# A banded attention and gated MLP on one core: the third tile's probabilities go through the DMA crossbar, and the low words of the weights are shifted in place

## The chip, the core and the metric
The kernel runs on one core of a Trainium2 chip. The core has TensorE (matmuls; "PE" in the profile, its weight loads "PEld"), VectorE (DVE), ScalarE (ACT), GpSimd (POOL) and SyncE (SP, which here only issues DMAs). They run at the same time and wait for each other by semaphores. SBUF is the working memory, PSUM the memory that TensorE writes. The metric is the device time of one execution in microseconds, median of the runs. Lower is better.

## What is computed
```
q, k, v: (8, 8, 576, 64)           # batch, heads, sequence, head size
scores = q @ k.T / sqrt(64) + slope[head] * -(i - j)     # only where 0 <= i - j < 128
attn   = softmax(scores) @ v       # (sum + 1e-9 in the denominator)
x      = attn as (4608, 512)       # tokens by heads * head size
h      = x @ w_in                  # (4608, 2048)
P = a0 + a1*h + a2*h^2 + a3*h^3
Q = 1 + |b0|*|h| + |b1|*h^2
out    = (P / (Q + 1e-6)) @ w_out  # (4608, 512), float32
```
All inputs and the output are float32, but w_in and w_out reach the kernel as 64-bit words (float64), which it converts itself.

## The kernel before
**Tiles.** The 4608 tokens are 36 blocks of 128 and 18 tiles of two blocks. Attention goes in steps: step j belongs to tile j // 2, and handles two of its four pairs of heads; one such pair is a "unit" (L508). A step's scores are 32 small matmuls (L466), 128 keys each, the window's two halves in `sc` and `side`; VectorE merges them (L491), adds the bias and takes the row maximum (L532), ScalarE takes the exponential and its sum (L537), VectorE the reciprocal of the sum (L544, L545), GpSimd scales (L546). The scaled probabilities `pr` must be transposed before the product with v (L417), which TensorE does in the same block as the next step's scores (L484).

**The transposition, in three ways (L563 to L591).** With j below DIRECT, TensorE transposes `pr` by four matmuls with a unit matrix (L561) and three operations pick from PSUM: ScalarE L580, VectorE L581 and L582. With j from DIRECT to below TURNED, TensorE transposes, ScalarE copies the whole (L586), and GpSimd makes the two parts (L589, L590). From TURNED on, ScalarE writes `pr` as two planes of 16-bit words (L566), SyncE issues a transposing DMA (L568: the crossbar), ScalarE puts the words together again (L569), and GpSimd makes the two parts. Before, step 4 goes the first way, step 5 the second, steps 6 to 35 the third.

**The weights (L608).** There are 32 pieces of 128 x 512 (16 of w_in, 16 of w_out), which arrive as `raw` of 512 KB, two 32-bit words an element, low and high. ScalarE turns the high words' exponent (a Prelu in place, L628). The low words are shifted right by 29 into a PSUM tile `cv` (L629), by ScalarE or by VectorE as the planner decides. VectorE shifts the high words left by 3 and joins the two (L630). The first tile uses these float32 weights. For the others each piece is split in a high and a low part: ScalarE casts (L642), VectorE or GpSimd subtracts (L643).

**The MLP (L649).** For two chunks of 128 of the 2048 columns at a time: up-projection (L667), the ratio P / Q by ScalarE (Abs L681, the affine part of P L686 or L697, Ln L690 or L701, Exp L691 or L702), GpSimd (Q: L683, L687 or L698) and VectorE (L688 to L707), then down-projection (L724), which adds up all 16 chunks in two PSUM banks `acc`. Lines L685 to L695 are the first tile's.

**The order.** Every operation is entered with a due time, the engines that may do it with a cost for each, and what it reads and writes (L98). The planner (L118) goes through a modelled time and gives each free engine the ready operation that is due first; the outcome is one fixed order for each engine (L780), which the chip's engines follow, each waiting where an operand isn't there. The due times come from constants (L297 to L304). VectorE's and GpSimd's operations marked `sb=True` are planned as excluding each other in time (L211, L231). The first tile's chunks, the conversions and splits and the first attention steps lie within the first 130 us. Small matmuls on constants (L760) fill TensorE until 19 us.
```
    if j >= TURNED:
        planes = slot(sb2, [P, 2, 4 * P], U16, "planes")
        turned = slot(sb2, [P, 8, P], U16, "turned")
...
    else:
        plan.op(A + (D2 if t else D0), {"p": 28 + 108 * 4}, transpose, ...)
```
Of the kernel before, what the change touches and what calls it, by code (L numbers as in the profile page):

```python
# [11 lines left out]
F32 = mybir.dt.float32  # L12
F32R = mybir.dt.float32r
BF16 = mybir.dt.bfloat16
I32 = mybir.dt.int32
U32 = mybir.dt.uint32
U16 = mybir.dt.uint16
AF = mybir.ActivationFunctionType
ALU = mybir.AluOpType
PSUM = bass.MemoryType.PSUM  # L20

P = 128
B, H, S, D = 8, 8, 576, 64
NT, DM, FF = B * S, H * D, 2048
# [10 lines left out]
MASKED = -8.0e9  # L35
GUARD = 1.0 + 1e-6
EARLY = 0
DIRECT = 5
TURNED = 6


def block_type(n):
# [239 lines left out]
def banded_attention_ratio_mlp(ctx: ExitStack, tc: tile.TileContext, kqv, w_in, w_out, ab, bias, ident, out):  # L282
    nc = tc.nc
# [6 lines left out]
    ps4 = ctx.enter_context(tc.tile_pool(name="ps4", bufs=4, space=PSUM))  # L290
# [3 lines left out]
    NJ = 2 * NTILE  # L294


    A0, DA, T0, L0, L1 = -20.125, 1.042, 19.836, 59.132, 26.846  # L297
    AOFF, D2, D3, JL, VL = -0.9676, 4.293, 7.221, 11.472, 6.149
    SP, SV, SA, SG, LL = 0.000768, 0.2712, 0.1218, 0.4427, 2.857
    ML, ZA, ME, OE, C0 = 24.839, 1.199, 1.338, 10.451, 0.4053  # L300
    DC, CO, DO, WL, S0 = 3.813, 18.57, 3.877, 4.536, 80.884
    DS, SL, AW, BL, VE = 1.477, 8.756, 26.824, 0.9349, 13.143
    DU, V0, DL, B2, B3 = 0.7375, 2.733, 1.877, 23.544, 56.47
    FE, D0, D4 = 19.023, 0.5665, 1.663  # L304

    plan = Plan({"p": 1000 * SP, "v": 1000 * SV, "a": 1000 * SA, "g": 1000 * SG})

    def slot(pool, shape, dtype, name, tag=None, view=None):
        return Slot(pool, count[id(pool)], shape, dtype, name, tag or name, view)

    def ap(s):
        if s.ap is None:
            s.ap = s.pool.tile(s.shape, s.dtype, name=s.name, tag=s.tag)
        return s.ap

    def act(n, psum, ptr=0):
        return (67 if psum else 105) + 0.833 * n + 95 * ptr
# [16 lines left out]
    guard, low_bias, tiny = fixed[:, 0:1], fixed[:, 1:2], fixed[:, 2:6]  # L334
# [38 lines left out]
    def c_time(k):  # L373
        return C0 + DC * (k // 2) if k % 2 == 0 else CO + DO * (k // 2)
# [133 lines left out]
    def unit(j, i, A, main, mk, pt, v):  # L508
# [53 lines left out]

        if j >= TURNED:  # L563
            planes = slot(sb2, [P, 2, 4 * P], U16, "planes")
# [10 lines left out]
        mixed = lambda: fresh(0)  # L575
        if j < DIRECT:
            picked = lambda y: slant(pt(), y)
# [6 lines left out]
            return  # L584
        if j < TURNED:
            plan.op(A + D2 + 0.2, {"a": act(4 * P, 1)}, lambda e: nc.scalar.copy(ap(w)[:, : 4 * P].rearrange("q (k h c) -> q k h c", k=2, h=2), pt()), reads=pk, writes=[(w, 0)])  # L586
# [21 lines left out]
    def convert(k):  # L608

        c, m = k // 2, k % 2  # L610
        f = slice(P * c, P * (c + 1))
        raw = raws[k] = slot(const, [P, 2 * DM], I32, f"raw{k}", tag=f"hi{k % NL}")
        bits = w32[c, m] = slot(const, [P, DM], F32, f"w32_{c}_{m}", tag=f"w{c}_{m}")
        T = c_time(k)
        cv_s = slot(ps4, [P, DM], I32, "cv", tag="h")
        ck = (cv_s, 0)
        cv = lambda: ap(cv_s)
        words = lambda: ap(raw).rearrange("p (a w) -> p a w", w=2)
        top, low = (lambda: words()[:, :, 1]), (lambda: words()[:, :, 0])

        def load(e):
            if m == 0:
                eng[e].dma_start(words().rearrange("p (k f) w -> p k f w", k=NKC), w_in[:, f, :].rearrange("(k p) f w -> p k f w", p=P))
            else:
                eng[e].dma_start(words(), w_out[f, :, :])

        plan.op(T - WL, {"s": 1450}, load, writes=[(raw, 0), (raw, 1)], after=1000 * (T - WL - 4), follows=[raws[k - NL]] if k >= NL else ())
        plan.op(T, {"a": 575}, lambda e: nc.scalar.activation(top().bitcast(F32), top().bitcast(F32), AF.Prelu, scale=2.0**-112, alpha=-(2.0**32)), writes=[(raw, 0)])  # L628
        plan.op(T, {"a": 640, "v": 603}, lambda e: nc.scalar.activation(cv(), low().bitcast(U32), AF.Relu, bias=low_bias, scale=2.0**-29) if e == "a" else nc.vector.tensor_single_scalar(cv(), low(), 29, op=ALU.logical_shift_right), reads=[(raw, 1)], writes=[ck])  # L629
        plan.op(T + 1, {"v": 603}, lambda e: nc.vector.scalar_tensor_tensor(ap(bits).bitcast(I32), top(), 3, cv(), ALU.logical_shift_left, ALU.bitwise_or), reads=[(raw, 0), ck], writes=[(bits, 0)])  # L630

    def split(c, m):

# [132 lines left out]
    for k in range(2 * NFC):  # L766
        convert(k)
# [62 lines left out]
```

## Time and profile before

| what | value |
|---|---|
| median of 3 runs | 978.71 us (977.4 to 979.03) |
| the profiled execution's own time | 978.76 us |
| its span, first to last instruction | 977.0 us |
| TensorE busy (share of the span) | 957.9 us (98%) |
| VectorE busy | 780.3 us (80%) |
| ScalarE busy | 704.0 us (72%) |
| GpSimd busy | 500.3 us (51%) |
| chain that ended last: TensorE's share | 38%, of it L724 18% and L667 17% |
| mean granted TensorE clock | 0.997 |

An engine's busy time says how long it had an instruction; for matmuls, which overlap, the ends are modelled. The granted clock is the share of TensorE's full speed that it was allowed. A row of the timeline gives start, duration, engine, line, operation, result <- operands, how many in a row, and in brackets how long the engine was idle before and what ended it. Two records of L724 or L667 in the first tile are one matmul in full float32. A line number is that of the kernel before; in the changed kernel the lines from L629 on stand one lower.

### The profile page before, as it was taken

What the parts mean: (1) busy time and instruction counts of PE and PEld (TensorE: products, weight loads), DVE (VectorE), ACT (ScalarE), POOL (GpSimd) and SP (SyncE); (2) the same over time, 40 slices, a digit from 0 to 9 for tenths busy, and PEclk for the clock granted to TensorE, in tenths of its full rate; (3) what the DMA queues carried; (4) which work ended last, traced back from release to release, by engine and by line L of the source; (5) the groups of instructions that cost most, each with busy time, mean ns of one, the idle gap of its engine ahead of it and who ended that gap; (6) DMA issues with size and microseconds to landing.
All of it is one profiled execution on the core that took longest, in us unless ns stands there. A gap on an engine that the chain in (4) does not pass through costs nothing. (4 is left out here: it accounts for less than half of the span.)

```text
span 977.0 us, 25069 instructions
## 1 busy us (share of the span) xinstructions
PE 957.9 (98%) x9838; PEld 846.8 (87%) x9838; DVE 780.3 (80%) x1803; ACT 704.0 (72%) x1482; POOL 500.3 (51%) x502
## 2 busy tenths in 40 slices
PE   9898999999999999999999999999999999999998
PEld 7665888899999999999898989989899999999997
DVE  6799888877788878787887778877887788878776
ACT  5888877777677777777767777777777776777653
POOL 0327774555455554555555545545555545554542
PEclk9999999999999999999999999999999999999999
DMA  8991213333333332232332333433222332321100
GB/s 277 363 337 53 77 46 91 79 77 93 78 88 81 89 77 84 70 98 78 82 80 52 71 103 77 93 77 77 71 71 78 77 84 64 92 72 45 23 22 21
DMA packets 117861, 89.57 MB, mean 92 GB/s; under 512 B 68848, under 2 KB 101872, under 8 KB 117744
## 3 DMA queue, kind: packets, MB, share of 16 engines
q1 hardware_dynamic: 117744, 87.98, 33.0%
q8 instruction: 77, 1.26, 0.6%
q14 instruction: 40, 0.33, 0.1%
HBM read 62.79 MB, written 9.44 MB: 74 GB/s over the span
## 5 line engine op out<-in xcount | busy, mean ns | idle before, releaser
L667 PE MATMUL h<-x_hi,hi 128*128 128x256 f32 x1088 | 308.5, 284 | 1.5 <-DVE x_lo L436 1.5
L667 PE MATMUL h<-x_lo,hi 128*128 128x256 f32 x1088 | 306.4, 282 | 0.0
L667 PE MATMUL h<-x_hi,lo 128*128 128x256 f32 x1088 | 306.2, 281 | 0.0
L667 PEld LDWEIGHTS h<-x_lo,hi 128*128 128x128 f32 x1088 | 205.3, 189 | 31.4 <-issue 0.7
L667 PEld LDWEIGHTS h<-x_hi,hi 128*128 128x128 f32 x1088 | 205.6, 189 | 20.7 <-issue 3.3
L724 PE MATMUL acc<-hi,g_h 128*128 128x512 f32 x544 | 215.5, 396 | 1.4 <-ACT o L752 1.4
L724 PE MATMUL acc<-lo,g_h 128*128 128x512 f32 x544 | 214.8, 395 | 0.0
L667 PEld LDWEIGHTS h<-x_hi,lo 128*128 128x128 f32 x1088 | 205.6, 189 | 0.0
L724 PE MATMUL acc<-hi,g_l 128*128 128x512 f32 x544 | 198.0, 399 | 1.3 <-DVE g_l L707 1.2
L683 POOL TENSOR_SCALAR g_q<-g_u,babs 128x512 f32<-128x512 f32 x136 | 107.5, 791 | 168.5 <-ACT g_u L681 157.6
L546 POOL TENSOR_TENSOR pr<-pr,st 128x512 f32<-128x512 f32 x70 | 78.7, 1127 | 221.2 <-DVE st L545 131.5
L698 POOL TENSOR_TENSOR g_q<-g_q,g_u 128x512 f32<-128x512 f32 x136 | 178.2, 1311 | 19.9 <-ACT g_q L683 10.8
L704 DVE SCALAR_TENSOR_TENSOR g_h<-h,ab_sb,g_u 128x512 fp32r<-128x512 f32 x136 | 101.4, 746 | 68.7 <-ACT g_u L702 68.3
L699 DVE TENSOR_TENSOR g_p<-h,g_p 128x512 f32<-128x512 f32 x136 | 93.5, 688 | 64.1 <-ACT g_p L697 50.3
L681 ACT ACTIVATE g_u<-h 128x512 f32<-128x512 f32 x144 | 86.1, 598 | 77.4 <-PE h L667 45.6
L537 ACT ACTIVATE pr<-pr,st 128x128 f32<-128x128 f32 x288 | 111.9, 391 | 39.8 <-DVE st L532 39.7
L697 ACT ACTIVATE g_p<-h,ab_sb 128x512 f32<-128x512 f32 x136 | 105.7, 779 | 45.0 <-PE h L667 44.7
L701 ACT ACTIVATE g_u<-g_q,fixed 128x512 f32<-128x512 f32 x136 | 98.3, 724 | 44.1 <-POOL g_q L698 43.9
L700 DVE SCALAR_TENSOR_TENSOR h<-g_p,ab_sb,h 128x512 f32<-128x512 f32 x136 | 102.3, 752 | 19.7 <-ACT g_u L681 17.8
L724 PEld LDWEIGHTS acc<-hi,g_h 128*128 128x128 f32 x544 | 102.6, 189 | 9.6 <-ACT o L752 1.8
L705 DVE SCALAR_TENSOR_TENSOR g_q<-g_q,g_h 128x512 f32<-128x512 f32 x136 | 105.9, 780 | 5.7
L724 PEld LDWEIGHTS acc<-hi,g_l 128*128 128x128 f32 x544 | 100.3, 188 | 11.1 <-DVE g_l L707 2.2
(82 smaller groups left out, 1561.6 us busy)
## 6 DMA issues: line engine op xcount, KB each, us to landing
kq<-in_kqv SPq DMA_DIRECT2D x72, 320.0 KB, 3.6
v<-in_kqv SPq DMA_DIRECT2D x144, 128.0 KB, 3.8
out<-o SPq DMA_DIRECT2D x34, 256.0 KB, 2.0
raw<-in_w_in SPq DMA_DIRECT2D x16, 512.0 KB, 8.5
raw<-in_w_out SPq DMA_DIRECT2D x16, 512.0 KB, 8.7
bias_t<-in_bias SPq DMA_DIRECT2D x44, 64.0 KB, 2.8
turned<-planes SPq DMA_TRANSPOSE x60, 3.1
out<-o SPq DMA_DIRECT2D x4, 128.0 KB, 1.7
```

What stands on the lines that cost most here:

```text
L537: nc.scalar.activation(ap(pr)[:, :, y, :], ap(pr)[:, :, y, :], AF.Exp, bias=ap(st)[:, y : y + 1], scale=-1.0, accum_out=ap(st)[:, 4 + y : ...
L667: nc.tensor.matmul(h(n), w[:, k, :], x[:, k, :], start=(k == 0 and m == 0), stop=(k == NKC - 1 and m == len(seq) - 1))
L681: plan.op(E, {"a": act(W, 1)}, lambda e: nc.scalar.activation(v(g_u), v(h_s), AF.Abs), reads=[(h_s, 0)], writes=[(g_u, 0)])
L683: lambda e: nc.scalar.activation(v(g_q), v(g_u), AF.Identity, bias=ap(babs)[:, 0:1], scale=ap(babs)[:, 1:2]) if e == "a" else nc.gpsimd.te ...
L697: plan.op(E, {"a": act(W, 1, 2) - 20}, lambda e: nc.scalar.activation(v(g_p), v(h_s), AF.Identity, bias=ap(ab_sb)[:, 2:3], scale=ap(ab_sb) ...
L698: plan.op(E, {"g": ttc}, lambda e: nc.gpsimd.tensor_tensor(v(g_q), v(g_q), v(g_u), ALU.mult), reads=[(g_q, 0), (g_u, 0)], writes=[(g_q, 0) ...
L699: plan.op(E, {"v": dve(W)}, lambda e: nc.vector.tensor_tensor(v(g_p), v(h_s), v(g_p), ALU.mult), reads=[(h_s, 0), (g_p, 0)], writes=[(g_p, ...
L700: plan.op(E, {"v": dve(W, 1)}, lambda e: stt(v(h_s), v(g_p), ap(ab_sb)[:, 1:2], v(h_s), ALU.add, ALU.mult), reads=[(h_s, 0), (g_p, 0), (ab ...
L701: plan.op(E, {"a": act(W, 0, 1)}, lambda e: nc.scalar.activation(v(g_u), v(g_q), AF.Ln, bias=guard, scale=1.0), reads=[(g_q, 0)], writes=[ ...
L704: plan.op(E, {"v": dve(W, 1)}, lambda e: stt(v(g_h), v(h_s), ap(ab_sb)[:, 0:1], v(g_u), ALU.add, ALU.mult), reads=[(h_s, 0), (g_u, 0), (ab ...
L705: plan.op(E, {"v": dve(W)}, lambda e: stt(v(g_q), v(g_q), GUARD, v(g_h).bitcast(F32), ALU.add, ALU.mult), reads=[(g_q, 0), (g_h, 0)], writ ...
L724: nc.tensor.matmul(ap(accs[t][i]), x[:, sl], w, start=(c == 0 and part == 0 and m == 0), stop=(c == NFC - 1 and part == parts - 1 and m == ...
```

## The change
Three things change.

DIRECT and TURNED become 4: steps 4 and 5, the third tile's, are transposed by the crossbar, as the later ones were.

In the conversion ScalarE's exponent pass writes to the PSUM tile `cv` instead of in place, the low words are shifted in place in SBUF, by VectorE alone, with `sb=True` and a planned cost of 336 instead of 603 ns, and VectorE joins `cv` with the shifted words.

All constants of the due times are others, so the planner's order differs on every engine and throughout.

```
--- before.py
+++ after.py
@@ -35,8 +35,8 @@
 MASKED = -8.0e9
 GUARD = 1.0 + 1e-6
 EARLY = 0
-DIRECT = 5
-TURNED = 6
+DIRECT = 4
+TURNED = 4
 
 
 def block_type(n):
@@ -294,14 +294,14 @@
     NJ = 2 * NTILE
 
 
-    A0, DA, T0, L0, L1 = -20.125, 1.042, 19.836, 59.132, 26.846
-    AOFF, D2, D3, JL, VL = -0.9676, 4.293, 7.221, 11.472, 6.149
-    SP, SV, SA, SG, LL = 0.000768, 0.2712, 0.1218, 0.4427, 2.857
-    ML, ZA, ME, OE, C0 = 24.839, 1.199, 1.338, 10.451, 0.4053
-    DC, CO, DO, WL, S0 = 3.813, 18.57, 3.877, 4.536, 80.884
-    DS, SL, AW, BL, VE = 1.477, 8.756, 26.824, 0.9349, 13.143
-    DU, V0, DL, B2, B3 = 0.7375, 2.733, 1.877, 23.544, 56.47
-    FE, D0, D4 = 19.023, 0.5665, 1.663
+    A0, DA, T0, L0, L1 = -22.674, 0.3976, 18.443, 59.244, 25.804
+    AOFF, D2, D3, JL, VL = -1.431, 3.98, 7.461, 11.098, 6.274
+    SP, SV, SA, SG, LL = 0.000768, 0.2712, 0.1218, 0.4427, 2.002
+    ML, ZA, ME, OE, C0 = 28.132, 1.085, 1.369, 7.847, 0.06437
+    DC, CO, DO, WL, S0 = 3.959, 18.781, 4.577, 4.421, 82.465
+    DS, SL, AW, BL, VE = 1.385, 7.772, 25.664, 1.141, 13.362
+    DU, V0, DL, B2, B3 = 0.7232, 2.957, 2.249, 23.312, 54.76
+    FE, D0, D4 = 19.132, 0.7658, 2.058
 
     plan = Plan({"p": 1000 * SP, "v": 1000 * SV, "a": 1000 * SA, "g": 1000 * SG})
 
@@ -612,9 +612,6 @@
         raw = raws[k] = slot(const, [P, 2 * DM], I32, f"raw{k}", tag=f"hi{k % NL}")
         bits = w32[c, m] = slot(const, [P, DM], F32, f"w32_{c}_{m}", tag=f"w{c}_{m}")
         T = c_time(k)
-        cv_s = slot(ps4, [P, DM], I32, "cv", tag="h")
-        ck = (cv_s, 0)
-        cv = lambda: ap(cv_s)
         words = lambda: ap(raw).rearrange("p (a w) -> p a w", w=2)
         top, low = (lambda: words()[:, :, 1]), (lambda: words()[:, :, 0])
 
@@ -625,9 +622,11 @@
                 eng[e].dma_start(words(), w_out[f, :, :])
 
         plan.op(T - WL, {"s": 1450}, load, writes=[(raw, 0), (raw, 1)], after=1000 * (T - WL - 4), follows=[raws[k - NL]] if k >= NL else ())
-        plan.op(T, {"a": 575}, lambda e: nc.scalar.activation(top().bitcast(F32), top().bitcast(F32), AF.Prelu, scale=2.0**-112, alpha=-(2.0**32)), writes=[(raw, 0)])
-        plan.op(T, {"a": 640, "v": 603}, lambda e: nc.scalar.activation(cv(), low().bitcast(U32), AF.Relu, bias=low_bias, scale=2.0**-29) if e == "a" else nc.vector.tensor_single_scalar(cv(), low(), 29, op=ALU.logical_shift_right), reads=[(raw, 1)], writes=[ck])
-        plan.op(T + 1, {"v": 603}, lambda e: nc.vector.scalar_tensor_tensor(ap(bits).bitcast(I32), top(), 3, cv(), ALU.logical_shift_left, ALU.bitwise_or), reads=[(raw, 0), ck], writes=[(bits, 0)])
+        cv_s = slot(ps4, [P, DM], I32, "cv", tag="h")
+        cv = lambda: ap(cv_s)
+        plan.op(T, {"a": 575}, lambda e: nc.scalar.activation(cv().bitcast(F32), top().bitcast(F32), AF.Prelu, scale=2.0**-112, alpha=-(2.0**32)), reads=[(raw, 0)], writes=[(cv_s, 0)])
+        plan.op(T, {"v": 336}, lambda e: nc.vector.tensor_single_scalar(low(), low(), 29, op=ALU.logical_shift_right), reads=[(raw, 1)], writes=[(raw, 1)], sb=True)
+        plan.op(T + 1, {"v": 603}, lambda e: nc.vector.scalar_tensor_tensor(ap(bits).bitcast(I32), cv(), 3, low(), ALU.logical_shift_left, ALU.bitwise_or), reads=[(cv_s, 0), (raw, 1)], writes=[(bits, 0)])
 
     def split(c, m):
 
```

Three places of the order follow. First ScalarE at the first tile's first ratios: `h` are the up-projections of chunks 0 to 3, `g_u` and `g_p` the ratio's parts, `raw` a weight piece. Before:
```order
L681 ACTIVATE g_u<-h 128x512
L686 ACTIVATE g_p<-h,na 128x512
L537 ACTIVATE pr,st<-pr,st 128x2x64 x3
L628 ACTIVATE raw_511<-raw_511 128x512
L681 ACTIVATE g_u<-h 128x512
L628 ACTIVATE raw_550<-raw_550 128x512
L690 ACTIVATE g_u<-g_q,fixed 128x512
L686 ACTIVATE g_p<-h,na 128x512
L691 ACTIVATE h<-g_u 128x512
```
and in the changed kernel:
```order
L680 ACTIVATE g_u<-h 128x512
L685 ACTIVATE g_p<-h,na 128x512
L537 ACTIVATE pr,st<-pr,st 128x2x64
L680 ACTIVATE g_u<-h 128x512
L685 ACTIVATE g_p<-h,na 128x512
L689 ACTIVATE g_u<-g_q,fixed 128x512
L690 ACTIVATE h<-g_u 128x512
```
The two exponent passes between the first Abs and the first Ln are gone from there, and the second chunk pair's affine (L685) stands ahead of the first Ln.

Second TensorE around the values of step 3 and the scores of step 4 (with tile numbers: `acc` the down-projection's banks, `w32_11_1` the eleventh piece of w_out, `pr_1080` and `pr_1033` the probabilities of step 3's second unit). Before:
```order
L724 MATMUL acc1_692<-w32_10_1_982,g_32_1050 128x512
L724 MATMUL acc0_678<-w32_11_1_1044,g_32_1050 128x512
L724 MATMUL acc1_692<-w32_11_1_1044,g_32_1050 128x512
L561 MATMUL sc_934<-id_sb_116,pr_1080 128x128 x4
L724 MATMUL acc0_678<-w32_12_1_1062,g_32_1155 128x512
L417 MATMUL side0_1173<-p_all_1078,v_803 64x128 x2
```
and in the changed kernel:
```order
L561 MATMUL sc_901<-id_sb_116,pr_1033 128x128 x4
L666 MATMUL h_1055<-x_hi_417,w32_15_0_993 128x256
L723 MATMUL acc1_689<-w32_9_1_996,g_32_936 128x512
L666 MATMUL h_1055<-x_hi_417,w32_15_0_993 128x256 x3
L417 MATMUL side0_1139<-p_all_1030,v_754 64x128 x2
...
L466 MATMUL side1_1142<-kq_573 64x64
L723 MATMUL acc0_678<-w32_10_1_1009,g_32_1133 128x512
```
The block of values and scores (L417, L466) now stands ahead of the down-projections of chunks 10, 11 and the first of 12, which were ahead of it.

Third ScalarE at the second tile's first ratios, after step 4's probabilities. Before:
```order
L681 ACTIVATE g_u<-h 128x512
L697 ACTIVATE g_p<-h,ab_sb 128x512
L683 ACTIVATE g_q<-g_u,babs 128x512
L580 COPY p_all<-sc 128x2x2x64
L642 CAST hi_1394<-w_9_0_778 128x512
L537 ACTIVATE pr,st<-pr,st 128x2x64 x4
L701 ACTIVATE g_u<-g_q,fixed 128x512 x2
L702 ACTIVATE g_u<-g_u 128x512 x2
```
and in the changed kernel:
```order
L680 ACTIVATE g_u<-h 128x512
L696 ACTIVATE g_p<-h,ab_sb 128x512
L682 ACTIVATE g_q<-g_u,babs 128x512
L566 COPY planes<-pr 128x1024
L569 COPY p_all<-turned 128x2x512
L700 ACTIVATE g_u<-g_q,fixed 128x512
L641 CAST hi_1435<-w_9_0_773 128x512
L701 ACTIVATE g_u<-g_u 128x512
```
Step 4's second plane copy (L566) and the copy back of its first unit (L569), which waits for the crossbar, now stand ahead of the second tile's first Ln (L700).

## Rows read from the trace of the kernel before

**Rows 1.** Busy time by stretches of the span: us, then for each engine the busy us and the instructions, the granted clock, the share of the 16 DMA engines, GB/s.
```profile
25.00:50.00 25.00, 20.86 (x153) 15.00 (x145) 19.23 (x49) 21.23 (x48) 8.15 (x8) 0.93 1.06 364
50.00:75.00 25.00, 23.70 (x196) 15.16 (x195) 24.85 (x49) 21.88 (x39) 6.17 (x6) 1.00 1.04 331
75.00:100.00 25.00, 21.89 (x202) 15.13 (x201) 23.43 (x54) 20.39 (x53) 20.15 (x17) 0.93 0.19 53
...
175.00:200.00 25.00, 25.00 (x288) 22.62 (x281) 19.66 (x48) 18.17 (x38) 12.99 (x15) 1.00 0.28 70
...
400.00:500.00 100.00, 99.57 (x1071) 90.26 (x1070) 80.42 (x190) 72.62 (x154) 53.13 (x54) 1.00 0.33 83
500.00:600.00 100.00, 99.07 (x1065) 89.36 (x1064) 78.11 (x187) 69.84 (x150) 50.08 (x53) 1.00 0.28 71
600.00:700.00 100.00, 99.55 (x1074) 89.97 (x1073) 79.71 (x192) 73.35 (x155) 52.02 (x56) 1.00 0.34 81
700.00:800.00 100.00, 100.00 (x1076) 90.81 (x1075) 80.33 (x189) 73.28 (x155) 54.64 (x55) 1.00 0.32 83
```

**Rows 2.** TensorE's timeline, 42 to 121 us.
```profile
42.37 4.54 PE L724 MATMUL acc<-w,g 128*128 128x512 f32 x6 [1.98 <-DVE g L695]
...
50.63 2.74 PE L724 MATMUL acc<-w,g 128*128 128x512 f32 x6
54.66 2.40 PE L667 MATMUL h<-x_hi,w 128*128 128x256 f32 x10 [1.30 <-DVE w L630]
...
88.29 0.66 PE L561 MATMUL sc<-id_sb,pr 128*128 128x128 f32 x4 [1.67 <-POOL pr L546]
90.39 2.08 PE L724 MATMUL acc<-w,g 128*128 128x512 f32 x2 [1.44 <-DVE g L695]
92.39 1.13 PE L417 MATMUL side<-p_all,v 64*64 64x128 f32 x16
...
104.61 1.02 PE L724 MATMUL acc<-w,g 128*128 128x512 f32 x2
105.47 0.60 PE L561 MATMUL sc<-id_sb,pr 128*128 128x128 f32 x4
105.83 0.37 PE L667 MATMUL h<-x_hi,hi 128*128 128x256 f32 x1
...
117.94 0.67 PE L417 MATMUL side<-p_all,v 64*64 64x128 f32 x16
```

**Rows 3.** Two stretches of 5 us, columns as in rows 1.
```profile
40.00:45.00 5.00, 3.02 (x8) 1.23 (x7) 4.96 (x18) 5.00 (x15) 2.20 (x3) 0.75 1.04 399
...
90.00:95.00 5.00, 4.61 (x94) 3.11 (x98) 5.00 (x8) 2.56 (x5) 4.13 (x4) 0.66 0.01 2
```

**Rows 4.** The timeline of ScalarE (33 to 39 us) and, last, of VectorE.
```profile
33.60 0.58 ACT L681 ACTIVATE g_u<-h 128x512 f32<-128x512 f32 x1
...
35.89 0.67 ACT L628 ACTIVATE raw<-raw 128x512 f32<-128x512 f32 x1
36.47 0.57 ACT L681 ACTIVATE g_u<-h 128x512 f32<-128x512 f32 x1
36.94 0.67 ACT L628 ACTIVATE raw<-raw 128x512 f32<-128x512 f32 x1
37.50 0.71 ACT L690 ACTIVATE g_u<-g_q,fixed 128x512 f32<-128x512 f32 x1
...
38.91 0.69 DVE L688 TENSOR_TENSOR g_p<-h,g_p 128x512 f32<-128x512 f32 x1 [2.04 <-ACT g_p L686]
```

**Rows 5.** VectorE's groups of instructions in the first 200 us: line, operation, result <- operands, shapes, count | busy us, mean ns of one | idle before.
```profile
L630 DVE SCALAR_TENSOR_TENSOR w<-raw,cv 128x512 int32<-128x512 int32 x32 | 21.1, 678 | 0.2 <-ACT cv L629 0.2
...
L629 DVE TENSOR_SCALAR cv<-raw 128x512 int32<-128x512 int32 x14 | 9.6, 689 | 0.8 <-DMA raw<-in_w_in 0.6
...
L643 DVE TENSOR_TENSOR lo<-w,hi 128x512 fp32r<-128x512 f32 x8 | 8.0, 1006 | 0.0
...
L544 DVE TENSOR_TENSOR st<-st,fixed 128x4 f32<-128x4 f32 x16 | 4.3, 270 | 0.4 <-ACT pr L537 0.4
...
L433 DVE COPY x_hi<-px 128x256 f32<-128x256 f32 x2 | 0.8, 424 | 0.2
L346 DVE CAST masks<-masks 128x256 f32<-128x256 bf16 x1 | 0.3, 295 | 4.1 <-DMA masks<-in_bias 4.1
```

**Rows 6.** The same view of ScalarE.
```profile
L629 ACT ACTIVATE cv<-raw,fixed 128x512 int32<-128x512 uint32 x18 | 13.1, 734 | 3.2 <-DVE w L630 2.2 <-DVE sc L491 0.9
...
L569 ACT COPY p_all<-turned 128x1024 uint16<-128x1024 uint16 x4 | 5.5, 1364 | 0.0
...
L566 ACT COPY planes<-pr 128x1024 uint16<-128x1024 uint16 x4 | 4.2, 1048 | 0.0
...
L580 ACT COPY p_all<-sc 128x256 f32<-128x256 f32 x6 | 2.3, 376 | 0.0
...
L586 ACT COPY p_all<-sc 128x512 f32<-128x512 f32 x2 | 1.1, 575 | 1.1 <-PE sc L561 1.1
```

**Rows 7.** VectorE's and GpSimd's timelines.
```profile
76.60 0.15 DVE L544 TENSOR_TENSOR st<-st,fixed 128x4 f32<-128x4 f32 x1
...
85.39 1.05 DVE L544 TENSOR_TENSOR st<-st,fixed 128x4 f32<-128x4 f32 x1
...
85.15 1.27 POOL L643 TENSOR_TENSOR lo<-w,hi 128x512 fp32r<-128x512 f32 x1
```

**Rows 8.** The crossbar's path of step 6's second unit, from ScalarE's plane copy to GpSimd's last operation, and ahead of it GpSimd's scaling of step 4's second unit.
```profile
110.21 1.04 POOL L546 TENSOR_TENSOR pr<-pr,st 128x512 f32<-128x512 f32 x1 [1.13 <-DVE st L545]
...
162.16 1.06 ACT L566 COPY planes<-pr 128x1024 uint16<-128x1024 uint16 x1
166.76 1.36 ACT L569 COPY p_all<-turned 128x1024 uint16<-128x1024 uint16 x1
...
169.02 1.07 POOL L590 TENSOR_TENSOR p_all<-p_all,p_far 128x256 f32<-128x256 f32 x1
```

## The prediction
> **What bounds the kernel now.** I read the busy time by stretches first. From 175 us on TensorE has no idle time to speak of: 25.00 of 25 us, 100.00 of 100 between 700 and 800, and 0.43, 0.93 and 0.45 us missing in the three hundreds between 400 and 700 [rows 1]. So the end is set by how much TensorE has to do and by what it lost before 175 us. There it waits for others: 4.1, 1.3 and 3.1 us are missing between 25 and 100 us, where VectorE is busy for 24.85 of 25 us (50 to 75) and 23.43 of 25 (75 to 100) [rows 1]. The timeline of TensorE then gives the places [rows 2]: it idles 1.98 us ahead of the first down-projection (42.37) and 1.44 us at 90.39, both for VectorE's last step of a ratio (L695), 1.30 us at 54.66 for a converted weight (L630), 1.67 us at 88.29 for a probability tile. [...]
>
> **TensorE's own work.** The third tile (attention steps 4 and 5) no longer has its 4 x 4 transposes on TensorE. A group of four at 105.47 has 0.60 us of records and is followed by the next matmul at 105.83, after 0.36 [rows 2]; matmuls overlap, so between the two I take 0.44 us, nearer to the distance: 4 x 0.44 = 1.8 us off an engine that is full afterwards. Bounds: 1.4 and 2.4. Two warming matmuls more (some 0.2 us) stand in front of the first real one, which waits for its operands anyway.
>
> **The first ratio, -3.8 us.** Before, ScalarE puts two weight conversions (35.89, 36.94) between the first chunk's Abs at 33.60 and its Ln at 37.50, and the second chunk's affine behind that; VectorE idles 2.04 us for it at 38.91 [rows 4]. In the changed order nothing of the conversion stands there (first fences above), because 18 shifts of 734 ns have left ScalarE [rows 6] and the exponent passes wait for later. At least two conversions of 0.56 us go (1.1 us), at most all of VectorE's 2.04. I take all: the 1.98 us at 42.37 go, and the 1.8 us of half clock behind them, since an engine that did not pause is not granted less in these rows. Bounds: 0 to -3.8.
>
> **VectorE's load, +1.0 us.** Before, 14 of 32 shifts run on VectorE into PSUM, 689 ns each, one every 0.60 us; the joining step L630 is as many and as long in both [rows 5]. Now all 32 run there, in SBUF. The trace has no such shift. The nearest rows: a cast of 256 elements from SBUF to SBUF takes 295 ns, a copy of 256 from PSUM 424 [rows 5]: 129 ns, half of 256 elements, less. For 512 that is 267 ns less than 689, so 0.42 us, one every 0.34. Between 0.34 and 0.60 I take 0.34, since the operand is in SBUF as the cast's is. Up to the first ratio (12 shifts now, 4 before) VectorE has idle time that takes them. Behind it: 20 x 0.34 - 10 x 0.60 = +0.8; step 4's four selections of 0.34 go (-1.3); two more weight splits (10, 8 before) come at 0.73 to 1.0 us (+1.5). Sum +1.0 in a stretch where VectorE ends the waits, so it counts in full. If shifts go at 0.60, it is +6.2.
>
> **Collisions with GpSimd, +2.3 us.** A small two-input step from SBUF (L544) takes 0.15 us when GpSimd is idle (76.60) and 1.05 us at 85.39, where it ends with GpSimd's split of 85.15 to 86.42 [rows 7]. So VectorE and GpSimd hold each other up over SBUF. If the in-place shift is of that kind, 20 shifts in the full stretch pay for it: L544's mean is 270 ns, 0.115 more than alone [rows 5, 7], and 20 x 0.115 = 2.3. Bounds: 0, and 20 x 0.55 (half of a 1.1 us operation each) = 11.
> [...]
>
> **ScalarE, GpSimd, SyncE.** ScalarE loses 18 x 734 ns and gains four plane copies (1048 ns) and four copies back (1364 ns) [rows 6], less 2 x 0.38 and 2 x 0.58 that go: net about -5.5 us, hidden as long as it is not the engine waited for. GpSimd has four operations like that of 1.07 us [rows 8] more for step 4 and two splits less. SyncE issues four transposes more, by the order between 100 and 140 us, where the raw weights have landed. All at nothing; what it costs if the cover goes is the first rival.
>
> **Later, -0.9 us.** The due times now run at 25.8 us per block, near the 25.5 that TensorE needs (values at 92.39 and 117.94 [rows 2]); before, at 26.8. In the new order the values steps stand at equal distances in TensorE's program. Of the 1.8 us missing from 400 to 700 I take half.
>
> **Sum.** -1.8 - 3.8 + 1.0 + 2.3 - 0.9 = -3.2 us. The profiled execution took 978.76 us (span 977.0), 0.05 more than the median of the runs: 975.5.
>
> **Rivals.**
> *The crossbar's path is late (slower).* Step 4's probabilities now go through GpSimd's scaling, a plane copy, SyncE's transpose, a copy back on ScalarE and two GpSimd operations; from the plane copy's start to the end of the last that is 169.02 + 1.07 - 162.16 = 7.9 us [rows 8]. The copy back stands ahead of the second tile's first Ln on ScalarE (third fences), so that ratio waits too. By the terms above TensorE comes to step 4's values at some 116.5 us (117.94, less two transpose groups, 3.8 - 1.0 - 2.3 = 0.5). It decides from a second scaling that begins after 116.5 - 7.9 - 1.1 = 107.5; before, it begins at 110.21 [rows 8]. Left there, TensorE waits 2.7 us, 1.4 for the copy in front of the Ln [rows 6], and some 2 at step 5, which goes the same way: +6 on 975.5, so 981.5. Against it: step 4's scores stand five down-projection matmuls and a transpose group earlier (second fences): three such matmuls are six records, 2.74 us [rows 2], so some 4.7 us.
> *Shifts at one element a cycle.* In place with every second word, 0.60 apart: +5.2, 980.7. For it: the only shift in the trace has 689 ns. Against it: the joining step reads the same words at 678 ns, no slower than others.
> [...]
> *VectorE gives the pause back.* The 3.8 us return as later waits for VectorE, full from 50 on: 975.5 + 3.8 - 0.9 = 978.4, no change.
> *No half clock anywhere.* If the pauses at 88 and 90 go too (3.1 us and 1.06 for a pair that takes 2.08 instead of 1.02 [rows 2]) and the collisions stay out: 975.5 - 4.2 - 1.3 = 970.
>
> **Chances.** Forecast 0.45 (its own range 972 to 977.5), pause given back 0.20, late crossbar 0.17, slow shifts 0.08, no half clock 0.10. The 8 in 10 range: 969.5 to 982.5. What this measurement tells from no change is 0.2%, 2 us: under 976.75 faster, over 980.67 slower. Faster: nine tenths of 0.45, and 0.10, so 0.51. Same: the rest of the forecast, the pause given back, some of the late crossbar: 0.27. Slower: 0.22.
>
> **What would show it.** Right: no pause and no half clock at 42 us; shifts near 0.42 us, a few over 1 us; eight transpose groups; TensorE at step 3's values (92.39 before) by some 87 us. Wrong: shifts near 0.69; TensorE waiting between 108 and 120 us for ScalarE's Ln or for GpSimd's last step of step 4; a half clock elsewhere in the first 130 us.

## The result: 0.68% slower

The changed kernel takes 984.71 us (median of 4 runs, 983.96 to 986.55) beside 978.06 before: ratio 1.0068, 95% interval 1.005 to 1.0085, so 6.7 us slower where I forecast 3.2 faster. The profiled execution is the slowest of the four (986.55, span 984.7), 1.84 us over the median.

The changed kernel's busy time by stretches, columns as in [rows 1]:
```profile
25.00:50.00 25.00, 19.98 (x167) 14.97 (x160) 21.97 (x55) 16.70 (x40) 8.38 (x8) 1.00 1.07 326
50.00:75.00 25.00, 20.72 (x178) 11.85 (x177) 24.29 (x54) 16.68 (x34) 4.09 (x4) 1.00 1.03 323
75.00:100.00 25.00, 21.90 (x196) 16.97 (x195) 21.38 (x53) 19.79 (x48) 21.03 (x18) 0.86 0.30 99
175.00:200.00 25.00, 25.00 (x271) 22.66 (x270) 20.84 (x49) 18.11 (x39) 14.86 (x16) 1.00 0.30 81
400.00:500.00 100.00, 100.00 (x1075) 90.49 (x1074) 79.97 (x191) 71.98 (x154) 51.26 (x55) 1.00 0.32 81
500.00:600.00 100.00, 98.39 (x1054) 88.87 (x1053) 77.97 (x185) 71.24 (x153) 50.94 (x54) 0.98 0.33 84
600.00:700.00 100.00, 100.00 (x1072) 90.51 (x1072) 78.49 (x188) 71.64 (x152) 51.29 (x54) 1.00 0.30 80
700.00:800.00 100.00, 100.00 (x1072) 90.35 (x1071) 78.76 (x180) 71.96 (x145) 53.58 (x56) 1.00 0.30 76
```
From 50 to 75 us TensorE is busy 20.72 us, before 23.70 [rows 1], while VectorE is as full (24.29) and ScalarE fell from 21.88 to 16.68: what ScalarE was relieved of helped nobody. TensorE's timeline gives the pauses:
```profile
42.46 2.84 PE L723 MATMUL acc<-w,g 128*128 128x512 f32 x6 [2.49 <-DVE g L694]
46.40 0.70 PE L666 MATMUL h<-x_hi,w 128*128 128x256 f32 x2 [1.10 <-DVE w L629]
...
57.31 2.74 PE L723 MATMUL acc<-w,g 128*128 128x512 f32 x6
61.60 1.98 PE L723 MATMUL acc<-w,g 128*128 128x512 f32 x4 [1.55 <-DVE g L694]
...
65.66 0.55 PE L417 MATMUL side<-p_all,v 64*64 64x128 f32 x10 [1.38 <-DVE w L629]
...
72.19 0.67 PE L666 MATMUL h<-x_hi,w 128*128 128x256 f32 x2 [0.86 <-DVE x_lo L436]
...
90.32 0.90 PE L417 MATMUL side<-p_all,v 64*64 64x128 f32 x10 [3.10 <-issue]
...
590.49 0.36 PE L666 MATMUL h<-x_hi,hi 128*128 128x256 f32 x1 [1.61 <-DVE x_lo L436]
```
The first one is still there, 2.49 us for 1.98 in [rows 2]. Those at 61, 65 and 72 are new. The 3.10 us at 90.32 are put down to "issue"; they end 0.10 us behind VectorE's last step of the sixth ratio:
```profile
89.53 0.69 DVE L694 SCALAR_TENSOR_TENSOR g<-g_q,h 128x512 f32<-128x512 f32 x1
```
L417's `side` tile takes its bank from the ring of four that `h` and `cv` use too, and this step is the last to read an `h`; so I read it as a wait for the bank. That was not tried by itself, but in each of the eight traces that have this pause (the changed kernel twice and, below, s_late_before, s_late_again, f_C, f_AC, s_unconvert, s_unconvert_late) it ends 0.10 us behind a ratio's last step.

Stretches of 5 us, to compare with [rows 3]:
```profile
40.00:45.00 5.00, 2.54 (x6) 1.06 (x6) 5.00 (x18) 4.27 (x14) 2.10 (x3) 1.00 1.10 267
90.00:95.00 5.00, 4.68 (x115) 4.71 (x119) 3.68 (x6) 3.46 (x7) 5.00 (x5) 0.50 0.02 3
...
590.00:595.00 5.00, 4.51 (x20) 4.20 (x21) 4.90 (x19) 4.17 (x13) 2.60 (x3) 0.66 0.81 229
```
The clock granted is 0.50 of full speed from 43 to 45 us before and from 91 to 95 here; I call that half clock. In this execution the half clock at 42 us has gone (1.00 for 0.75), that at 90 has grown (0.50 for 0.66), and one stands behind the pause at 590 (0.66). These places are not fixed. In a second trace of the same kernel (after_again, below) the clock is 1.00 from 90 to 95 and from 590 to 595 us, and 0.66 from 65 to 70; and the first stretch and the first records read:
```profile
40.00:45.00 5.00, 2.33 (x7) 1.05 (x6) 5.00 (x17) 3.99 (x13) 2.40 (x3) 0.75 1.10 296
```
```profile
43.10 4.23 PE L723 MATMUL acc<-w,g 128*128 128x512 f32 x6 [2.67 <-DVE g L694]
...
57.96 2.74 PE L723 MATMUL acc<-w,g 128*128 128x512 f32 x6
```
It costs no time there: from the first down-projection to the six records at 57.96 it is 14.86 us, without the half clock 14.85 (42.46 to 57.31), since the wait of 1.10 us at 46.40 is then not there.

**TensorE's deficit.** To see where time is lost, I give each matmul record the distance at which its kind follow each other where nothing waits (0.119 us for L666, 0.231 for L723, 0.215 and 0.43 for their float32 halves in the first tile, 0.11 for a transpose, 0.023 for the small ones of L417 and L466) and subtract the work begun from the time. What grows is waiting and half clock. us, at five times, for the profiled executions:

| kernel | 60 | 95 | 120 | 200 | 960 |
|---|---|---|---|---|---|
| before | 24.0 | 29.2 | 30.4 | 34.5 | 42.6 |
| changed | 22.9 | 33.8 | 35.3 | 39.7 | 52.2 |
| f_C (new constants only) | 23.7 | 27.0 | 28.3 | 37.0 | 46.9 |
| s_late_again (late order of before) | 22.9 | 33.4 | 34.7 | 39.1 | 48.1 |
| s_convert (conversion in the order of before) | 26.2 | 32.1 | 35.3 | 39.8 | 46.9 |
| s_allv (32 shifts on VectorE to PSUM) | 28.1 | 33.0 | 38.0 | 43.2 | 51.0 |
| s_mixed_here (14 pieces changed) | 24.2 | 30.1 | 32.4 | 36.5 | 44.0 |
| s_cross (crossbar in the order of before) | 23.5 | 28.7 | 34.4 | 46.7 | 54.2 |

The changed kernel gains 1.1 us until 60, loses 5.7 from 60 to 95 (10.9 for 5.2; from 60 to 75 alone it is 5.4 for 0.1), 0.6 to 200, 4.4 after 200 (12.5 for 8.1), and has 1.8 us less to do: 7.8, the spans' 7.7.

### The profile page after: what moved, and what is told of

It reads as the page before. It is cut to its first block, busy times and chain, and to the rows that moved or that the text cites. A ratio compares the mean times of both kernels' runs of the same rounds, so it can differ in the third digit from the quotient of the medians.

```text
span 984.7 us, 25114 instructions
## 1 busy us (share of the span) xinstructions
PE 960.6 (98%) x9824; PEld 847.4 (86%) x9824; DVE 779.9 (79%) x1818; ACT 696.7 (71%) x1468; POOL 497.6 (51%) x505
## 3 DMA queue, kind: packets, MB, share of 16 engines
q1 hardware_dynamic: 121968, 89.03, 33.8%
## 4 chain that ended last, share of the span: by engine, by line
PE 86%; DVE 5%; ACT 4%; DMA 3%; issue 2%; SPq 1%; DVEq 0%; ACTq 0%
PE acc L723 38%; PE h L666 38%; PE side L417 5%; PE sc L466 3%; DMA raw<-in_w_in 2%; PE side L466 1%; DMA turned<-planes 1%; ACT hi L641 1%; DVE w L629 1%; DMA kq<-in_kqv 1%; DVE raw L628 1%; ACT pr L537 1%; DVE g L694 0%; ACT g_q L682 0%; ACT o L751 0%
## 5 line engine op out<-in xcount | busy, mean ns | idle before, releaser
L666 PE MATMUL h<-x_hi,hi 128*128 128x256 f32 x1088 | 310.0, 285 | 3.5 <-DVE x_lo L436 2.5
L666 PE MATMUL h<-x_lo,hi 128*128 128x256 f32 x1088 | 307.0, 282 | 0.0
L666 PE MATMUL h<-x_hi,lo 128*128 128x256 f32 x1088 | 307.0, 282 | 0.0
L666 PEld LDWEIGHTS h<-x_lo,hi 128*128 128x128 f32 x1088 | 205.4, 189 | 35.2 <-issue 2.2
L666 PEld LDWEIGHTS h<-x_hi,hi 128*128 128x128 f32 x1088 | 206.0, 189 | 26.2 <-issue 5.9
L723 PE MATMUL acc<-hi,g_h 128*128 128x512 f32 x544 | 217.6, 400 | 0.3
L723 PE MATMUL acc<-lo,g_h 128*128 128x512 f32 x544 | 215.0, 395 | 0.0
L666 PEld LDWEIGHTS h<-x_hi,lo 128*128 128x128 f32 x1088 | 205.8, 189 | 0.0
L723 PE MATMUL acc<-hi,g_l 128*128 128x512 f32 x544 | 202.4, 398 | 0.0
L546 POOL TENSOR_TENSOR pr<-pr,st 128x512 f32<-128x512 f32 x70 | 74.6, 1066 | 244.2 <-DVE st L545 133.3
L697 POOL TENSOR_TENSOR g_q<-g_q,g_u 128x512 f32<-128x512 f32 x136 | 181.1, 1333 | 14.5 <-ACT g_q L682 5.6
L700 ACT ACTIVATE g_u<-g_q,fixed 128x512 f32<-128x512 f32 x136 | 98.6, 725 | 45.3 <-POOL g_q L697 45.3
L723 PEld LDWEIGHTS acc<-hi,g_h 128*128 128x128 f32 x544 | 102.8, 189 | 9.4 <-ACT o L751 1.6
L723 PEld LDWEIGHTS acc<-lo,g_h 128*128 128x128 f32 x544 | 102.2, 188 | 7.0
```

The lines of the kernel that those rows point to most:

```text
L666: nc.tensor.matmul(h(n), w[:, k, :], x[:, k, :], start=(k == 0 and m == 0), stop=(k == NKC - 1 and m == len(seq) - 1))
L697: plan.op(E, {"g": ttc}, lambda e: nc.gpsimd.tensor_tensor(v(g_q), v(g_q), v(g_u), ALU.mult), reads=[(g_q, 0), (g_u, 0)], writes=[(g_q, 0) ...
L700: plan.op(E, {"a": act(W, 0, 1)}, lambda e: nc.scalar.activation(v(g_u), v(g_q), AF.Ln, bias=guard, scale=1.0), reads=[(g_q, 0)], writes=[ ...
L723: nc.tensor.matmul(ap(accs[t][i]), x[:, sl], w, start=(c == 0 and part == 0 and m == 0), stop=(c == NFC - 1 and part == parts - 1 and m == ...
```

## The experiments

**One part at a time, order worked out anew.** A is DIRECT and TURNED, B the conversion, C the constants, each as in the diff of the change; f_A is the kernel before with A, and so on.
```
-DIRECT = 5
-TURNED = 6
+DIRECT = 4
+TURNED = 4
```


> The kernel before with the third tile's transposes on the crossbar and nothing else (DIRECT and TURNED 4; conversion and constants of before). Three theories of the 6.6 us: the order that the new constants make (O), the in-place shift and its collisions with GpSimd (S), the crossbar's path (X). O and S: 1 to 2 us faster than before, since four transpose groups of 0.44 us go. X: 4 us or more slower.

Measured: 1.0139 [1.0097, 1.018].

> The kernel before with the changed conversion and nothing else (transposes and constants of before). S: 5 to 8 us slower than before. O and X: within 2 us of before. VectorE's shifts near 0.42 us with some over 0.8, mean 0.53, in any case.

Measured: 1.0174 [1.0141, 1.0207].

> The kernel before with the new constants of the due times and nothing else. O: 4 to 8 us slower than before, with a pause of TensorE between 85 and 95 us at step 3's values. S and X: within 2 us of before.

Measured: 1.0057 [1.0041, 1.0073]; a pause of 2.10 us stands inside step 3's values, at 90.03.

> The changed kernel with the constants of before. O: within 2 us of before or 1 to 3 us faster, so 5 us or more faster than the changed kernel. S or X: 3 us or more slower than before.

Measured: 1.0103 [1.0065, 1.0141].

> The changed kernel with the conversion of before, the order worked out anew from the new constants. S: 4 to 5 us faster than the changed kernel, if the new order does not take it back elsewhere; each order worked out anew with constants made for other operations has cost 6 to 18 us so far, so 984 or more is the likelier.

Measured: 1.011 [1.0095, 1.0126].

Each part alone is slower, by 6 to 17 us, and so are two together (of the three pairs B with C was not run), and no theory holds alone: every change of operations or constants gives a new order throughout, and an order from constants that were not made for the operations costs as much as anything in the diff. To tell operations from order, the order had to be held. In the kernels below (s_...) the planner is replaced by a written list of operations with their engines; their lines stand 3 to 9 higher.
```
-    order = plan.order()
+    order = json.loads(zlib.decompress(base64.b64decode(ORDER)))
     with tc.manual_schedule():
-        for o in order:
-            o.emit(o.engine)
+        for i, e in order:
+            warming(e) if i < 0 else plan.ops[i].emit(e)
```

**The late order.** The operations after 190 us are the same in both kernels; only their order differs. `late` are the operations from step 7's values on:
```
-order_of_changed
+[x for x in order_of_changed if x not in late] + [x for x in order_of_before if x in late]
```

> The changed kernel with all its operations; the order of each engine is the changed kernel's until about 190 us (the block of step 7's values) and from there on the kernel before's, written out as a list. The late theory (L: some 4.4 us of the loss come from the order after 200 us, in a stage whose operations the change does not touch): 980 us, 4 to 5 faster than the changed kernel. The early theory (E: all is lost before 130 us, and what is late only shifts): 984 to 985, as the changed kernel.

Measured: 984.13, 1.0061 [1.004, 1.0083], beside 1.0068 for the changed kernel in another comparison: no difference shown.

> The kernel before with all its operations; the order of each engine is its own until about 190 us and the changed kernel's from there on. L: 4 to 5 us slower than before, about 983. E: as before, within 1.5 us.

Measured: 981.15, 1.0026 [1.0011, 1.004], so 2.5 us slower.

Since the two disagreed, both kernels ran again side by side:

> The changed kernel once more, beside the next: 984 to 985 us by both theories.

> The changed kernel with the order of before from about 190 us on, once more, on the same chip as the changed kernel. L (the later order costs): 2 to 4 us faster than the changed kernel. E (it does not): the same within 1 us.

Measured: 985.56, 1.0072 [1.0058, 1.0087], and 981.89, 1.0036 [1.0023, 1.0049]. The intervals do not meet: here the late order costs 3.7 us. s_late_again is s_late_before's program unchanged, which lay only 0.6 us under the changed kernel of another comparison, and s_late_after gave 2.5; so I put the cost at 2 to 4 us, an estimate. (The 4.4 of the deficit include a half clock at 590 us that not every execution has, as the last section shows; in after_again's trace the same growth is 2.2 above that of before.) Not all of it can be seen in the traces: TensorE's pauses after 190 us add up to 2.5 us in after_again and to 2.4 in s_late_again. The pause at 590 goes with the late order; TensorE's timeline of s_late_after, where L670 is the up-projection, has it too:
```profile
587.46 0.35 PE L670 MATMUL h<-x_hi,hi 128*128 128x256 f32 x1 [1.61 <-DVE x_lo L439]
```
and the stretch from 500 to 600 us, in after_again, then in s_late_again:
```profile
500.00:600.00 100.00, 98.39 (x1064) 88.81 (x1064) 79.65 (x189) 71.34 (x153) 51.34 (x54) 1.00 0.33 84
```
```profile
500.00:600.00 100.00, 99.66 (x1074) 90.15 (x1073) 78.83 (x188) 70.64 (x150) 49.51 (x52) 1.00 0.31 74
```

**The conversion in the order of before.** Where the exponent pass stood, VectorE shifts in place; where the shift stood, ScalarE does the pass to PSUM:
```
-(prelu[k], "a") ... (shift[k], engine_of_before)
+(shift[k], "v") ... (prelu[k], "a")
```

> The kernel before in its own order, with the changed conversion put into it: where the exponent pass stood VectorE now shifts in place, where the shift stood ScalarE now does the exponent pass to PSUM; nothing else moves. If the conversion itself makes VectorE late (S): 3 to 6 us slower than before (18 shifts more on VectorE, some waiting for GpSimd). If the loss before 130 us is only a matter of the new order (O): within 2 us of before, and the prediction's two terms for VectorE (1.0 and 2.3 us) would be the most of it.

Measured: 1.0054 [1.0035, 1.0072], 5.3 us slower. VectorE's shifts in the first 200 us, and two of TensorE's waits (L697 is the ratio's last step, L726 the down-projection):
```profile
L631 DVE TENSOR_SCALAR raw<-raw 128x512 int32<-128x512 int32 x32 | 15.5, 487 | 0.7 <-DMA raw<-in_w_in 0.4
```
```profile
43.87 2.84 PE L726 MATMUL acc<-w,g 128*128 128x512 f32 x6 [2.84 <-DVE g L697]
...
94.21 2.08 PE L726 MATMUL acc<-w,g 128*128 128x512 f32 x2 [1.52 <-DVE g L697]
```
The first ratio's last step starts 1.5 us later than before (43.1 for 41.6), the eighth's 4.0 (98.5 for 94.5). Three rivals for this cost followed: VectorE's time, the PSUM bank, the place.

s_allv is before's own conversion, all 32 shifts to PSUM on VectorE:
```
-[(i, e) for i, e in order_of_before]
+[(i, "v" if i in shifts else e) for i, e in order_of_before]
```


> The kernel before in its own order with its own conversion, but all 32 shifts on VectorE, from SBUF to PSUM at one every 0.60 us. V: 18 x 0.60 = 10.8 us more on VectorE, of which idle time ahead of the first ratio takes 2 to 4: 7 to 9 us slower than before, so slower than s_convert. I: no in-place shift and no meeting with GpSimd, so within 3 us of before.

Measured: 1.0086 [1.0071, 1.0102], 8.4 us slower; the eighth ratio is 7.8 us late (102.3). No shift here is in place, and in the trace of before GpSimd stretched no shift to PSUM: the 14 on VectorE take 0.68 to 0.70 us, the six that begin during an instruction of GpSimd among them. So work added to VectorE alone does it.

s_mixed converts as s_convert the 14 pieces whose shift VectorE had anyway:

> The kernel before in its own order; only the 14 pieces whose shift VectorE did take the changed conversion (VectorE shifts in place, ScalarE's exponent pass to PSUM), the 18 others keep ScalarE's shift. VectorE's load theory (V: what costs is the time that the conversion takes on VectorE in the stretch where it is full): 14 x 0.26 = 3.6 us less on VectorE, 1 us or so given back to GpSimd: 1 to 3 us faster than before. If an in-place shift or the exponent pass to PSUM is what costs (I): 14/32 of s_convert's 5.3, so 2 us slower.

Measured: 1.003 [1.0019, 1.0041], 2.9 us slower, against the theory that bore out in s_allv. So the swapped places were undone:
```
-swap(prelu[k], shift[k])
+move(prelu[k], ahead_of=shift[k])
```


> s_mixed with another place: for the 14 pieces both the exponent pass to PSUM and the in-place shift stand where the shift stood in the kernel before, so VectorE meets no shift whose weights have not landed. If s_mixed lost by that place (P): as before or up to 2 us faster. If the PSUM bank that ScalarE's exponent pass must wait for is what costs (B), or meeting GpSimd (G): 2 to 3 us slower than before, as s_mixed.

Measured: 0.9997 [0.9983, 1.0011]. The swap was s_mixed's cost, though not by weights that had not landed: VectorE waits for those 1.7 us there and 1.5 here, but for ScalarE's Exp of the ratios 1.3 and 0.4. Of the 3.6 us that 14 shifts should save, 1.4 come (one every 0.50 us in the mean for 0.60, idle time left out): four meet GpSimd (0.62 to 1.52 us each). Two wait for weights besides. So a conversion that moves nothing onto VectorE is worth nothing here. s_convert moves 18 shifts there and has the swapped places as well, for all 32 pieces; how much of its 5.3 us is the one and how much the other was not separated.

Without the bank, exponent pass and shift both in place, the join from SBUF:
```
-top(), 3, cv(), ALU.logical_shift_left, ALU.bitwise_or
+top(), 3, low(), ALU.logical_shift_left, ALU.bitwise_or
```


> The kernel before, every instruction in its place; for the 14 pieces VectorE's shift is in place in SBUF, the exponent pass stays in place too, and the join reads both from SBUF, so these pieces use no PSUM bank. VectorE's work falls by up to 14 x 0.26 = 3.6 us. P or B: 1 to 3 us faster than before. G: shifts and joins that meet GpSimd eat it up, within 1 us of before or slower.

Measured: 1.0006 [0.9993, 1.002].

> The kernel before in its order; all 32 shifts on VectorE in place, the exponent pass in place, the join from SBUF, no PSUM bank for any piece. VectorE's load theory (V): 32 x 0.34 - 14 x 0.60 = 2.5 us more and the meetings with GpSimd, 3 to 6 us slower than before, as s_convert. B: the bank was the cost of s_convert, so within 2 us of before.

Measured: 1.011 [1.0084, 1.0137]. The bank is not the cost. VectorE's join (L633) and shift (L632) here:
```profile
L633 DVE SCALAR_TENSOR_TENSOR w<-raw 128x512 int32<-128x512 int32 x32 | 23.3, 747 | 0.1
L632 DVE TENSOR_SCALAR raw<-raw 128x512 int32<-128x512 int32 x32 | 19.3, 616 | 0.0
```
The shift is 616 ns in the mean for 424 alone, and the join from SBUF 747 for 678 [rows 5]; I read that as more meetings with GpSimd. The eighth ratio is later (102.1), and so is the end. On every engine the order is that of s_allv, so shifts that are cheaper alone gained nothing over shifts to PSUM (10.8 us slower, there 8.4).

**The crossbar in the order of before.**
```
-(transpose, "p"), (copy, "a"), (near, "v"), (far, "v")
+(planes, "a"), (turn, "s"), (back, "a"), (far, "g"), (rest, "g")
```

> The kernel before in its own order, with the third tile's transposes on the crossbar: the sixteen groups' 4 x 4 matmuls go, the plane copies stand right behind the scaling, the copies back 3.7 us behind the transposing DMA. If the path through the crossbar is hidden: 1 to 2 us faster than before. If it is late (X): TensorE waits at step 4's or 5's values, and the time is the same or up to 4 us slower.

Measured: 1.0103 [1.008, 1.0127], 10 us slower. GpSimd's last operation for step 4 and TensorE's values of the second unit:
```profile
123.70 1.18 POOL L593 TENSOR_TENSOR p_all<-p_all,p_far 128x256 f32<-128x256 f32 x1
...
124.93 0.49 PE L420 MATMUL side<-p_all,v 64*64 64x128 f32 x4 [2.50 <-POOL p_all L593]
```
That is the late path of my first rival, though only 2.5 of the 10 us are this wait: TensorE also waits 1.8 us at 114.13 for a copy of ScalarE and 1.9 us at 161.93 for an `x_lo`, and runs at half clock from 115 to 120 (0.50). What those have to do with the crossbar was not taken apart. In the changed kernel the same pair has 4.4 us to spare (117.98 to 122.34):
```profile
117.25 0.73 POOL L590 TENSOR_TENSOR p_all<-p_all,p_far 128x256 f32<-128x256 f32 x1
...
122.34 0.82 PE L417 MATMUL side<-p_all,v 64*64 64x128 f32 x14
```

**The conversion out of the changed order.** The reverse of s_convert's edit, on the changed kernel's list (and in the second kernel on that of s_late_again):
```
-(shift[k], "v") ... (prelu[k], "a")
+(prelu[k], "a") ... (shift[k], engine_of_before)
```

> The changed kernel in its own order with the conversion of before put back: where VectorE shifted in place ScalarE does the exponent pass in place, where ScalarE did its pass to PSUM stands the shift to PSUM, on ScalarE for the same 18 pieces as in the kernel before and on VectorE for 14. If the conversion is the early loss in this order too (S): 4 to 5 us faster than the changed kernel, about 980. If the early loss is this order's (O): within 2 us of the changed kernel.

Measured: 1.0085 [1.007, 1.0099].

> The same with the order of before from about 190 us on as well; the third tile's transposes stay on the crossbar. S and L together: 984.7 less 5 less 3.7, about 976, so 2 us faster than before (the four transpose groups). O: 980 to 981.

Measured: 1.0058 [1.0044, 1.0072]. Neither is faster than the changed kernel with the same late order; the late order is worth 3.1 us by the medians here too. The time of the first does not tell the early theories apart: the exponent pass now stood close ahead of the join, and VectorE waited 5.0 us for it (8 times). Its trace says more, as the next section shows.

## Why the prediction was wrong, step by step

**TensorE's own work: right.** 32 transposing records where there were 48, four groups of four less, and the waits of TensorE from 100 to 200 us name nothing of the crossbar's path; the deficit grows by 5.9 us from 95 to 200, before by 5.3. But the cover is TensorE's own lateness: by the prediction step 4's values were due at 116.5, and the path ends at 117.98. The crossbar by itself, in the changed order, was not tried.

**The first ratio, -3.8: the step that failed first.** "I take all: the 1.98 us at 42.37 go." ScalarE's two conversions did leave, but VectorE's queue got shifts in their place, which I had counted as filling idle time. The last step of the ratio's part on ScalarE (the Exp, L690), VectorE up to the ratio's last step, and GpSimd beside it:
```profile
37.47 0.60 ACT L690 ACTIVATE h<-g_u 128x512 f32<-128x512 f32 x1
```
```profile
37.38 0.65 DVE L687 TENSOR_TENSOR g_p<-h,g_p 128x512 f32<-128x512 f32 x1
37.95 0.97 DVE L628 TENSOR_SCALAR raw<-raw 128x512 int32<-128x512 int32 x1
38.85 0.73 DVE L688 SCALAR_TENSOR_TENSOR g_p<-g_p,na,h 128x512 f32<-128x512 f32 x1
39.50 0.84 DVE L628 TENSOR_SCALAR raw<-raw 128x512 int32<-128x512 int32 x1
40.26 0.68 DVE L691 SCALAR_TENSOR_TENSOR g_q<-g_q,h 128x512 f32<-128x512 f32 x1
40.86 0.74 DVE L692 SCALAR_TENSOR_TENSOR h<-g_p,na,h 128x512 f32<-128x512 f32 x1
41.52 0.28 DVE L532 CUSTOM_DVE_ANT_0 pr<-sc,bias_std 128x128 f32<-128x128 f32 x1
41.73 0.08 DVE L532 DVE_READ_ACCUMULATOR2_ANT st<- 128x1 f32 x1
41.73 0.68 DVE L694 SCALAR_TENSOR_TENSOR g<-g_q,h 128x512 f32<-128x512 f32 x1
```
```profile
37.60 1.04 POOL L546 TENSOR_TENSOR pr<-pr,st 128x512 f32<-128x512 f32 x1 [0.17 <-DVE st L545]
38.60 1.46 POOL L686 TENSOR_TENSOR g_q<-g_q,g_u 128x512 f32<-128x512 f32 x1
```
Two shifts of 0.97 and 0.84 us (0.42 alone) stand inside the chain, each stretched by GpSimd. The Exp is done at 38.07, but VectorE comes to L691, which reads it, at 40.26; the two shifts push it back by 1.66 us (37.95 to 38.85, 39.50 to 40.26). So the pause did not go (2.49 us for 1.98). The half clock went in two of the four traces with this early order (in this one and s_late_before, not in after_again and s_late_again), which is luck, and where it stayed it cost 0.0 and 0.3 us by the six records at 57; the term has 1.8 for it, six records of 4.54 us at 42.37 less six of 2.74 at 50.63 [rows 2]. So next to nothing of the 3.8 us came. The 1.1 us gained by 60 us are about the wait of 1.30 at 54.66 [rows 2], which is gone.

**VectorE's load and the collisions, +1.0 and +2.3: prices right, but the time went by the order, which the sum has at nothing here.** The conversion's two operations on VectorE:
```profile
L629 DVE SCALAR_TENSOR_TENSOR w<-cv,raw 128x512 int32<-128x512 int32 x32 | 21.4, 680 | 0.5 <-ACT cv L627 0.2
L628 DVE TENSOR_SCALAR raw<-raw 128x512 int32<-128x512 int32 x32 | 16.5, 531 | 2.7 <-DMA raw<-in_w_in 2.6
```
A shift alone takes 0.42 us, as worked out (median 424 ns); the mean of 531 puts the collisions at 32 x 0.107 = 3.4 us. That GpSimd holds up a shift in place as it does L544 was assumed in the 2.3 us, since no shift of before is in place and so no row there shows the term; here seven of the 32 are held up (last section). GpSimd waits too: its split L642 takes 1.27 us at 94.65, with VectorE idle, and 1.73 at 84.22, where it begins during VectorE's split of 83.69 (1.12 us). The prices thus held, but the 12 early shifts were not free (first ratio), and TensorE lost 5.7 us more than before between 60 and 95. Nearly all of that falls between 60 and 75 us; from 85 to 95 the deficit grows by 5.6, before by 5.1. VectorE is not late in that stretch: the last steps of the second to the fifth ratio start at 45.0, 52.5, 60.9 and 66.8, before at 48.3, 55.7, 61.2 and 68.6. The pauses go with the order. Growth of the deficit from 60 to 75 us:

| order | conversion of before | changed conversion |
|---|---|---|
| of before, held | 0.1 (before) | 0.4 (s_convert) |
| worked out anew | 0.1 each (f_A, f_C, f_AC) | 7.6 (f_B), 8.0 (f_AB) |
| of the changed kernel, held | 6.2 (s_unconvert), 6.1 (s_unconvert_late) | 5.4 (changed), 6.1 (after_again) |

s_unconvert, with the conversion of before, pauses where the changed kernel does at 61.60 and 65.66:
```profile
62.52 1.98 PE L727 MATMUL acc<-w,g 128*128 128x512 f32 x4 [1.20 <-DVE g L698]
...
66.56 0.55 PE L420 MATMUL side<-p_all,v 64*64 64x128 f32 x10 [1.42 <-DVE w L633]
```
Its own waits for the exponent pass lie before 28 us and after 69, outside these two. So this loss comes with the order that the planner makes for the changed conversion, not with the price of the operations. In TensorE's row one sees that 6 records of up-projections begin between 60 and 75 us, before 20. Load on VectorE alone can cost there too, but less: s_allv, with 10.8 us more on VectorE in the order of before, loses 2.4. Which places of the new order cost it was not tried; nor does the table say what the 0.86 us at 72.19 belong to, since s_unconvert has waits of its own by then. s_convert loses as much as the changed kernel does early, but elsewhere: 2.2 us by 60, and 4.9 by 120.

**Later, -0.9: wrong in sign.** Equal distances between the values steps are no gain by themselves; the late order costs some 2 to 4 us, in a stage that the change does not touch. I had read the order there only in its due times, not in what stands next to what: the pause at 590 is an up-projection too close behind the `x_lo` it needs. What the rest of the cost is stays open.

**The signs.** Shifts near 0.42 us (24 of 32), eight transpose groups and the start of step 3's values at 86.78 came as forecast. But those values then stood until 90.32, the pause at 42 was there, and so was a half clock elsewhere in the first 130 us, at 90.

**The rivals.** The late crossbar had the right sign and a wrong mechanism for this kernel. Slow shifts, one every 0.60 us, did not come: the median is 0.42 us, and 24 of the 32 take 0.40 to 0.43. The pause given back had later waits for VectorE, which came, but in return for 3.8 us that had never been gained. No half clock anywhere did not happen; its sum takes off 1.3 for the collisions, which the forecast prices at 2.3. No rival had an order that loses time by itself.

## What to carry to other kernels

Work moved from an engine with room to the one that ends the waits cost here about the time that it took there, collisions included, even where each piece had become cheaper alone. In the order of before, the 18 shifts of s_allv put 10.8 us more on VectorE and cost 8.4; s_sbuf's shifts (one every 0.54 us) and slower joins put 10.9 us more there, by estimate from the rows above, and cost 10.8. A place in the queue cost time too: s_mixed's 2.9 us are the swap. So count pieces times price on the full engine, from the first piece on, and do not take idle time for free before you have seen what stands behind it in the queue. Where a planner sets the order, a change of operations is also a change of order everywhere; hold the order as a list to tell the two apart, and splice lists to see which stretch of an order loses. No version here beats the kernel before: s_mixed_here, the nearest, can't be told from it.

## What was not expected of the hardware

A shift in place that met GpSimd waited for the whole of GpSimd's instruction: both shifts above end 0.28 us behind it (38.92 and 38.64, 40.34 and 40.06), and all seven shifts of this trace that begin during an instruction of GpSimd end 0.28 to 0.29 us behind its end, while L688 between them, which has an operand in PSUM, runs at its usual 0.73 us beside GpSimd.

The clock did not follow the length of one pause: it stayed at 1.00 behind 2.49 us at 42, and fell behind the same 2.49 us in s_late_again, whose order is the same until 190 us (0.85 from 40 to 45 us). Behind a pause of 1.61 us at 590 it fell to 0.66 in the profiled execution above, and behind the same pause it stayed at 1.00 in after_again:
```profile
590.00:595.00 5.00, 4.86 (x33) 4.52 (x34) 4.89 (x17) 3.84 (x13) 2.62 (x3) 1.00 0.75 231
```
